# One sum and one reciprocal for a pair of heads, and a fixed place in the load queue for late weights and keys

## Chip, cores and metric

The kernel runs on one core of one Trainium2 chip. The metric is the device time of an execution in microseconds (us). The engines are PE (TensorE, matmuls), DVE (VectorE), ACT (ScalarE), POOL (GpSimd) and SP (SyncE, which here issues all loads and stores as one queue).

## The reference

Four batches with eight heads each: 512 local and 32 global queries and keys, head size 64. Local queries see the 32 global keys and the local keys within 32 positions; global queries see all keys. Then two MLPs over 2176 rows of 512.

```
s_g = scale * q_g @ k_all.T;   out_g = softmax(s_g) @ v_all
s_l = scale * [q_l @ k_g.T, where(|i - j| <= 32, q_l @ k_l.T, -1e9)]
out_l = softmax(s_l) @ [v_g, v_l]
x = rows of all heads side by side                    # 2176 x 512
h = maximum(x @ w_in, 0);      x2 = (h * h) @ w_out     # 512 -> 2048 -> 512
y = ((x2 @ w1) * (x2 @ w2)) @ w3 @ w_out2               # 512 -> 1024 -> 512
```

softmax here subtracts the row's maximum, takes exp, and divides by the sum plus 1e-9.

## The kernel before, in words

Heads go in 16 pairs j (heads 2j and 2j + 1); pairs 0 to 3 are batch 0, and so on. `emit_s(j, part)` makes the local scores of both heads of a pair for one half of the queries (part 0 or 1): for each head two tiles `sc`, 192 and 224 keys wide. `soft(i, part, sc)` (L235) turns one head's scores into probabilities `p`: for each tile DVE adds the mask, scales and takes the least (L245), and ACT takes the exponential and its row sum into `st` (L249). Then DVE adds each sum and the 1e-9 beside it (L253), takes the reciprocal (L254), and multiplies both tiles with it (L257). PE transposes `p` (`emit_t`, L332), ACT copies the result to `pt` (L334, L337), and PE multiplies it with v (`emit_pv`, tile `o`, L159); ACT copies `o` to `xb` (L363) and casts it to the high part `hl` (L584), DVE makes the low part (L154). The five `p` buffers and six `st` tiles are used in turn.

`emit_g(j)` does the 32 global queries of both heads at once: scores `sg` (L165), two maxima (L300), the larger of them (L303), its product with minus the scale (L304), exp on ACT (L306), sum, reciprocal and product (L309 to L311, tile `pg`), then transposes (`tg`, L319).

The MLP is in three products of high and low parts. First `h` (L165) from `hl` and the weights `u`, then `x` or `acc` (L165, L633). Later stages, with lines from L830 on, form both further products. Raw weights are 64-bit words, loaded by `load_w` (L447, `n` counts them) and converted in steps: two on ACT (L453, L456), two on DVE (L464, L469), an add on POOL (L536), a cast on ACT (L477) and a subtraction on DVE (L478). Attention of batch b + 1 runs beside the first MLP of batch b, and the conversions of units 0 to 15 beside both.

Keys and queries of pair j come by `load_kq` (L197): for pairs 4 to 7 straight into the tile that is used, for pairs 8 to 15 (j >= NATIVE) into `kqraw`, two buffers, which DVE splits into high and low parts (cast L228, subtraction L154, `kq_hl`).

What sets the order: the program is written as lists of steps that are merged, and a scheduler then orders the instructions of each engine by its own model of their times. An instruction under `tc.keep_in_program_order` keeps its place among those of its engine that are so marked. Each engine then runs its list strictly in order. All loads and stores are on one list too, that of SP; an issue waits until its tile is free or its data are there, and the issues behind it wait with it.

Of the kernel before, what the change touches and what calls it, by code (L numbers as in the profile page):

```python
# [9 lines left out]
F32 = mybir.dt.float32  # L10
F32R = mybir.dt.float32r
BF16 = mybir.dt.bfloat16
I32 = mybir.dt.int32
U32 = mybir.dt.uint32
AF = mybir.ActivationFunctionType
ALU = mybir.AluOpType
AX = mybir.AxisListType
# [4 lines left out]
S = SL + SG  # L22
# [3 lines left out]
SCALE = 0.125  # L26
# [13 lines left out]
NK = KPOS.size  # L40
KSTART = (0, 96, 256, 320)
# [3 lines left out]
REACH = ((0, 192), (96, 320), (256, 480), (384, 576))  # L45
SLOT = (0, 1, 1, 0)
WIDTH, AT, PW = (192, 224), (288, 0), 544
# [10 lines left out]
HALF = 256  # L58
# [12 lines left out]
RUNS = (0, 16, PAIRED + 16)  # L71
# [4 lines left out]
HEAD, FEW = 4, 2  # L76
# [31 lines left out]
NATIVE = 8  # L108
# [6 lines left out]
AT_BUFS, H_BUFS, X_BUFS, P_BUFS, KQ_BUFS, ST_BUFS, HL_BUFS = 4, 2, 2, 5, 4, 6, 14  # L115
# [3 lines left out]
def attention_mlp(ctx: ExitStack, tc: tile.TileContext, kq0, kq, vw, wts, mask, ident, out_d):  # L119
    nc = tc.nc  # L120
# [9 lines left out]
    cv, rot, at = cv_cm.__enter__(), rot_cm.__enter__(), at_cm.__enter__()  # L130
# [4 lines left out]
    mask_sb = rot.tile([128, 4, 256], BF16, name="mask_sb")  # L135
# [4 lines left out]


    p_all = [rot.tile([128, PW], F32, name=f"p{k}") for k in range(P_BUFS)]
    sts = [rot.tile([128, 10], F32, name=f"st{k}") for k in range(ST_BUFS)]
    stgs = [rot.tile([64, 8], F32, name=f"stg{k}") for k in range(2)]
    xs_d = dram.tile([128, 4, 2, NT], F32, name="xs_d")
    part_d = dram.tile([128, 4, NT], F32, name="part_d")
# [9 lines left out]
    def in_turn(products, whole):  # L156

        for k, (o, w, x, start, stop) in enumerate(products):
            m = mm(o, w, x, start=start, stop=stop)  # L159
            if k or whole:  # L160
                tc.keep_in_program_order(m)

    def chain(o, terms):
        for k, (w, x) in enumerate(terms):
            mm(o, w, x, start=(k == 0), stop=(k == len(terms) - 1))  # L165
# [16 lines left out]
    kq_raw, kq_t, v_t, p_t, pt_t = {}, {}, {}, {}, {}  # L182

    def kq_tile(name, dtype=F32):
        return rot.tile([128, S + NK], dtype, tag="kq", name=name, bufs=KQ_BUFS)
# [11 lines left out]
    def load_kq(j):  # L197

        if H <= 2 * j < B * H:
            if j < NATIVE:  # L200
                t = kq_tile("kq_f32")
            else:
                t = pools["cv"].tile([128, S + NK], F32, tag="kqraw", name="kqraw", bufs=2)
            kq_raw[j] = t
            for h, r in enumerate(ROWS):
                src = kq[2 * j + h - H, r]
                nc.sync.dma_start(out=t[r, :HALF], in_=src[:, :HALF])
                nc.sync.dma_start(out=t[r, HALF:S], in_=src[:, HALF + NK :])
                nc.sync.dma_start(out=t[r, S:], in_=src[:, HALF : HALF + NK])

    def load_v(i, part=None):

# [19 lines left out]
            kq_t[j, part] = [(both[a][0], both[e][1]) for a, e in PASSES]  # L232
        load_kq(j + 1)

    def soft(i, part, sc):  # L235

        p = p_all[0]
        p_all.append(p_all.pop(0))
        st = sts[(2 * i + part) % ST_BUFS]
        least, sums, over = st[:, 0:2], st[:, 2:6].rearrange("p (n k) -> p n k", k=2), st[:, 6:8]  # L240
        for t in range(2 * part, 2 * part + 2):
            n = SLOT[t]
            c, w = slice(AT[n], AT[n] + WIDTH[n]), slice(0, WIDTH[n])
            m = slice(REACH[t][0] - KSTART[t], REACH[t][1] - KSTART[t])
            nc.vector.tensor_tensor_reduce(  # L245
                out=p[:, c], in0=sc[:, n, w], in1=mask_sb[:, t, m], scale=-SCALE,
                scalar=3.0e38, op0=ALU.add, op1=ALU.min, accum_out=least[:, n : n + 1],
            )
            nc.scalar.activation(  # L249
                p[:, c], p[:, c], AF.Exp, bias=least[:, n : n + 1], scale=-1.0,  # L250
                accum_out=sums[:, n, 0:1],
            )
        nc.vector.tensor_reduce(out=over, in_=sums, axis=AX.X, op=ALU.add)  # L253
        nc.vector.reciprocal(over, over)  # L254
        for n in range(2):
            c = slice(AT[n], AT[n] + WIDTH[n])
            nc.vector.tensor_scalar_mul(p[:, c], p[:, c], over[:, n : n + 1])  # L257
        p_t[i, part] = p

    def emit_s(j, part):  # L260

        terms = kq_t[j, part]
        sc = [ps.tile([128, 2, 256], F32, tag="at", name="sc", bufs=AT_BUFS) for _ in ROWS]
        at_q, at_t = (128 * n + SG * part for n in range(2)), range(2 * part, 2 * part + 2)
        in_turn(
            (
                (o[:, n, : WIDTH[n]], x[r, c : c + 128], y[r, slice(*REACH[t])], k == 0, k == len(terms) - 1)
                for c, t, n in ((c, t, SLOT[t]) for c, t in zip(at_q, at_t))
                for k, (x, y) in enumerate(terms) for o, r in ((sc[h], ROWS[h]) for h in HEADS)
            ),  # L270
            j >= WHOLE,
        )
        for h, o in enumerate(sc):
            soft(2 * j + h, part, o)

    def emit_g(j):

        terms = kq_t[j, 1]
        qs = qgf if len(terms) == 1 else [qgp[:, 0], qgp[:, 0], qgp[:, 1]]
        for q, (x, _) in list(zip(qs, terms))[:: 2]:  # L280
            for h, r in enumerate(ROWS):
                nc.gpsimd.tensor_copy(q[r, SG * h : SG * (h + 1)], x[r, :SG])
        bank = dict(tag="x", bufs=X_BUFS) if j < APART else dict(tag="at", bufs=AT_BUFS)
        sg = [ps.tile([128, 512], F32, name="sg", **bank) for _ in range(2)]

        pf = pg.rearrange("p c k -> p (c k)")
        tail = pf[:, 288:736].rearrange("p (a c) -> p a c", a=2)[:, :, :128]
        pieces = (
            (sg[0][:, :288], lambda x: x[:, :288], pf[:, :288]),
            (  # L290
                sg[1][:, :256].rearrange("p (a c) -> p a c", a=2),
                lambda x: x[:, 256:576].rearrange("p (a c) -> p a c", a=2)[:, :, 32:160],
                tail,
            ),
        )
        for k, (s, of_keys, _) in enumerate(pieces):
            chain(s, [(q, of_keys(y)) for q, (_, y) in zip(qs, terms)])
        st = stgs[j % 2]
        for k in range(2):
            nc.vector.tensor_reduce(  # L300
                out=st[:, k : k + 1], in_=sg[k][:64, : 256 + 32 * (1 - k)], axis=AX.X, op=ALU.max
            )
        nc.vector.tensor_reduce(out=st[:, 2:3], in_=st[:, 0:2], axis=AX.X, op=ALU.max)  # L303
        nc.vector.tensor_scalar_mul(st[:, 2:3], st[:, 2:3], -SCALE)  # L304
        for k, (s, _, p) in enumerate(pieces):
            nc.scalar.activation(  # L306
                p[:64], s[:64], AF.Exp, bias=st[:, 2:3], scale=SCALE, accum_out=st[:, 3 + k : 4 + k]
            )
        nc.vector.tensor_reduce(out=st[:, 6:7], in_=st[:, 3:6], axis=AX.X, op=ALU.add)  # L309
        nc.vector.reciprocal(st[:, 6:7], st[:, 6:7])  # L310
        nc.vector.tensor_scalar_mul(pf[:64, :640], pf[:64, :640], st[:, 6:7])  # L311
# [77 lines left out]
    def cycle(j, ahead=True, behind=True):  # L389
# [3 lines left out]
        if ahead:  # L393
            s.append(lambda: (emit_k(n) if n == H // 2 else None, emit_g(n)))
            s += [lambda part=part: emit_s(n, part) for part in ((1,) if native else (0, 1))]
# [39 lines left out]
    def load_w(n):  # L435
        if n < RUNS[1]:
            t = unit("u1", I32).rearrange("p a c -> p (a c)").rearrange("p (c w) -> p c w", w=2)
        elif n % 3 == 2:
            t = extra["w"][:, :1024].bitcast(I32).rearrange("p (c w) -> p c w", w=2)
        else:  # L440
            t = pools["cv"].tile([128, 512, 2], I32, tag="wraw", name="wraw", bufs=2)
        if n >= PAIRED:
            k, u = divmod(n - PAIRED, 2)
            at = PAIRED + 2 * (LATE + FIRST)[k] + u
        else:
            at = ORDERED[n] if n < RUNS[1] else n
        nc.sync.dma_start(out=t, in_=wts[at].bitcast(I32).rearrange("p (c w) -> p c w", w=2))  # L447
        raw_t[n] = t

    def conv_a(n):  # L450
# [22 lines left out]
    def unit(tag, dtype=F32R):  # L473
        return pools[tag].tile([128, 2, 512], dtype, tag=tag, name=tag, bufs=16)
# [239 lines left out]
    def end_a(i, d, o):  # L714
        (nc.scalar.copy if d < 2 or i < SHARED else nc.vector.tensor_copy)(staged(i, d), o)
        if d == 3:
            nc.sync.dma_start(out=of(part_d, i), in_=st_t[0])

    def split_a(i, d):
        if i < NBLK:  # L720
            split_x(i, d, xcols(i)[:, d])
        else:
            load_split(0, d, 2)
# [20 lines left out]
    for i in range(0, NBLK, 2):  # L744
        main = []
        for j in (i, i + 1):
            if j >= SHARED:
                if j == SHARED:
# [3 lines left out]
                    lambda d, j=j: split_a(j + 1, d), lambda d, j=j: end_a(j, d, acc[d]),  # L752
# [15 lines left out]
        else:  # L768
# [9 lines left out]
            for j in range(FEW):  # L778
# [3 lines left out]
                    lambda d, j=j: end_few(j, d),  # L782
# [190 lines left out]
    for i in range(NBLK):  # L973
# [3 lines left out]
            lambda d, i=i: end_b(i, d), 0 if i < NBLK - 1 else 4,  # L977
# [243 lines left out]
```

## Time and profile before

| | |
|---|---|
| median of 3 runs | 853.44 us (851.83 to 854.47) |
| profiled execution, device time | 852.59 us |
| its span, first to last instruction | 850.8 us |
| mean granted clock of PE | 0.994 of 2.4 GHz |
| busy: PE, DVE, ACT, POOL | 826.6, 587.9, 491.1, 216.5 us |
| loads and stores | 151.96 MB, 54.0% of the 16 DMA engines' time in the main queue |

A row of the page gives an engine's busy time and the number of its instructions. A timeline gives each instruction's start and length; instructions of one kind in a row are merged to one line with their number. In square brackets stands how long the engine was idle before, and what ended that. The chain of work that ended last is, for its last 86 us, PE alone.

### The profile page before, as it was taken

Reading aid. Unit: us, or ns where it says so; the run is one execution under the profiler, and the core shown is the slowest. Engines: PE = TensorE matmul, PEld = TensorE weight load, DVE = VectorE, ACT = ScalarE, POOL = GpSimd, SP = SyncE. Lnnn points to the kernel's source line nnn. Section 1 sums busy time; section 2 is a strip of 40 time slices with the busy share of each in tenths; the row PEclk is TensorE's granted clock in tenths of the full one; section 3 lists DMA queues with packets and bytes.
Section 4 is the critical chain, followed back from the end, with each engine's and each line's share of the span. In section 5 each row is a group of like instructions: output and inputs, shape, how many; then the busy total and the mean of one; then the engine's idle time right before and its main releaser. Section 6 shows DMA issues by size and latency. Waiting matters only on the chain. (4 is left out here: it accounts for less than half of the span.)

```text
span 850.8 us, 17854 instructions
## 1 busy us (share of the span) xinstructions
PE 826.6 (97%) x6624; PEld 787.8 (93%) x6624; DVE 587.9 (69%) x1611; ACT 491.1 (58%) x1323; POOL 216.5 (25%) x256
## 2 busy tenths in 40 slices
PE   6789799999999999999999999999999999999998
PEld 4578689999999999999999999999999999999998
DVE  7878986773866576877662027796896757789862
ACT  7778876664766787777664246776411212255650
POOL 3401222000200233333331003330277454442000
PEclk9999999999999999999999999999999999999999
DMA  9964313424051685875854239745347543939931
GB/s 335 262 197 144 114 54 118 133 78 127 29 174 33 228 279 180 284 253 182 252 153 157 69 120 330 248 167 174 128 140 242 195 145 111 333 114 331 336 142 54
DMA packets 89879, 151.96 MB, mean 179 GB/s; under 512 B 6336, under 2 KB 63296, under 8 KB 89792
## 3 DMA queue, kind: packets, MB, share of 16 engines
q1 hardware_dynamic: 89792, 150.82, 54.0%
q8 instruction: 52, 0.85, 0.4%
q14 instruction: 35, 0.29, 0.1%
HBM read 103.42 MB, written 47.38 MB: 177 GB/s over the span
## 5 line engine op out<-in xcount | busy, mean ns | idle before, releaser
L165 PE MATMUL h<-hl,u 128*128 128x288 f32 (+1 forms) x1536 | 229.3, 292 | 2.6 <-ACT hl L584 1.1
L165 PEld LDWEIGHTS h<-hl,u 128*128 128x128 f32 x1536 | 205.6, 190 | 8.6 <-ACT hl L584 1.3
L830 PE MATMUL m<-hl,u 128*128 128x272 f32 x1296 | 170.9, 288 | 0.9 <-DVE r L852 0.9
L830 PEld LDWEIGHTS m<-hl,u 128*128 128x128 f32 x1296 | 165.3, 188 | 1.4 <-ACT hl L866 1.1
L633 PE MATMUL acc<-hl,u 128*128 128x256 f32 (+1 forms) x1032 | 149.0, 288 | 0.2 <-DVE hl L154 0.2
L633 PEld LDWEIGHTS acc<-hl,u 128*128 128x128 f32 x1032 | 137.6, 188 | 1.2 <-DVE hl L154 0.4
L154 DVE TENSOR_TENSOR hl<-r,hl 128x288 fp32r<-128x288 f32 (+1 forms) x128 | 80.1, 630 | 73.8 <-ACT r L604 72.6
L536 POOL TENSOR_TENSOR wt<-wt 128x512 int32<-128x512 int32 x56 | 74.0, 1322 | 213.6 <-DVE wt L469 72.6
L599 ACT ACTIVATE r<-h 128x288 f32<-128x288 f32 (+1 forms) x128 | 49.9, 393 | 75.4 <-PE h L165 74.2
L165 PE MATMUL x<-hl,u 128*128 128x288 f32 (+1 forms) x504 | 74.0, 294 | 0.0
L847 ACT COPY r<-m 128x272 f32<-128x272 f32 x40 | 15.4, 385 | 101.0 <-PE m L830 96.1
L249 ACT ACTIVATE p<-p,st 128x192 f32<-128x192 f32 (+1 forms) x128 | 59.0, 464 | 19.5 <-DVE st L245 19.3
L830 PE MATMUL m<-u,u 128*128 128x272 f32 x528 | 70.0, 287 | 0.0
L165 PEld LDWEIGHTS x<-hl,u 128*128 128x128 f32 x504 | 66.6, 189 | 2.5 <-issue 1.3
L830 PEld LDWEIGHTS m<-u,u 128*128 128x128 f32 x528 | 67.2, 188 | 0.3 <-DVE rs L854 0.2
L478 DVE TENSOR_TENSOR u<-wt,u 128x512 fp32r<-128x512 f32 x56 | 40.3, 719 | 29.6 <-ACT u L477 29.0
L600 ACT ACTIVATE hl<-r 128x288 fp32r<-128x288 f32 (+1 forms) x128 | 54.8, 432 | 4.2 <-PE acc L633 1.5
L1023 POOL TENSOR_TENSOR rs<-rs 128x272 f32<-128x272 f32 x64 | 55.7, 881 | 3.2
L1022 POOL TENSOR_TENSOR rs<-rs 128x272 f32<-128x272 f32 x32 | 28.7, 898 | 98.9 <-DVE rs L860 98.9
L245 DVE CUSTOM_DVE_ANT_0 p<-sc,mask_sb 128x192 f32<-128x192 f32 (+1 forms) x128 | 40.8, 368 | 14.6 <-PE sc L159 14.5
L469 DVE SCALAR_TENSOR_TENSOR wt<-wt 128x512 int32<-128x512 int32 x72 | 49.6, 689 | 1.7
L526 POOL TENSOR_TENSOR u<-wt 128x512 int32<-128x512 int32 x16 | 22.5, 1410 | 99.0 <-DVE wt L469 81.9
(113 smaller groups left out, 1271.0 us busy)
## 6 DMA issues: line engine op xcount, KB each, us to landing
wraw<-in_wts SPq DMA_DIRECT2D x37, 512.0 KB, 4.3
q_d<-rs SPq DMA_DIRECT2D x16, 952.0 KB, 4.6
rl<-q_d SPq DMA_DIRECT2D x12, 1088.0 KB, 7.4
wx<-in_wts SPq DMA_DIRECT2D x19, 512.0 KB, 5.1
u<-in_wts SPq DMA_DIRECT2D x16, 512.0 KB, 6.3
v_f<-in_vw SPq DMA_DIRECT2D x24, 256.0 KB, 3.0
hl<-xs_d SPq DMA_DIRECT2D x20, 288.0 KB, 4.4
hl<-xs_d SPq DMA_DIRECT2D x20, 256.0 KB, 4.3
```

Source lines behind the costliest of these rows:

```text
L154: eng.tensor_tensor(out=lo, in0=raw, in1=hi.bitcast(F32), op=ALU.subtract)
L165: mm(o, w, x, start=(k == 0), stop=(k == len(terms) - 1))
L245: nc.vector.tensor_tensor_reduce(out=p[:, c], in0=sc[:, n, w], in1=mask_sb[:, t, m], scale=-SCALE, scalar=3.0e38, op0=ALU.add, op1=ALU.min ...
L249: nc.scalar.activation(p[:, c], p[:, c], AF.Exp, bias=least[:, n : n + 1], scale=-1.0, accum_out=sums[:, n, 0:1],)
L469: nc.vector.scalar_tensor_tensor(out=b, in0=a, scalar=-(1 << 31), in1=b, op0=ALU.bitwise_and, op1=ALU.bitwise_or)
L478: s = nc.vector.tensor_tensor(out=t[:, 1, cols], in0=raw, in1=t[:, 0, cols].bitcast(F32), op=ALU.subtract)
L536: nc.gpsimd.tensor_tensor(out=b, in0=b, in1=m, op=ALU.add)
L599: nc.scalar.activation(r, h, AF.Relu)
L600: nc.scalar.activation(g[:, 0], r, AF.Square)
L633: mm(acc[d], w[:, a, 128 * d : 128 * (d + 1)], g_t[f][:, b], start=(f + k == 0), stop=(last and k == 2),)
L830: mm(o, w, x, start=(i in (1, 6, 5, 4) and k == 0), stop=(k == len(terms) - 1), skip_group_check=(i in (2, 7, 3)),)
L1023: sub = lambda o, a, c: nc.gpsimd.tensor_tensor(out=o, in0=a, in1=c, op=ALU.subtract)
```

## The change

`soft` now takes a pair, not a head. The four tiles of the two heads have their four row sums in one `st` tile, sixteen columns wide instead of ten; one sum over all four and one reciprocal follow, then the four multiplications. In `emit_g`, the larger of two maxima and its product with minus the scale become one instruction. Loads of raw weights 8 to 15 and of the keys of pairs 8 to 15 are marked to keep the program's order. The diff, without lines that only carry a new argument:

```diff
-    sts = [rot.tile([128, 10], F32, name=f"st{k}") for k in range(ST_BUFS)]
+    sts = [rot.tile([128, 16], F32, name=f"st{k}") for k in range(ST_BUFS)]
...
-                nc.sync.dma_start(out=t[r, :HALF], in_=src[:, :HALF])
-                nc.sync.dma_start(out=t[r, HALF:S], in_=src[:, HALF + NK :])
-                nc.sync.dma_start(out=t[r, S:], in_=src[:, HALF : HALF + NK])
+                q, k = slice(0, HALF), slice(HALF, HALF + NK)
+                for to, c in ((q, q), (slice(HALF, S), slice(HALF + NK, None)), (slice(S, None), k)):
+                    d = nc.sync.dma_start(out=t[r, to], in_=src[:, c])
+                    if j >= NATIVE:
+                        tc.keep_in_program_order(d)
...
-    def soft(i, part, sc):
-
-        p = p_all[0]
-        p_all.append(p_all.pop(0))
-        st = sts[(2 * i + part) % ST_BUFS]
-        least, sums, over = st[:, 0:2], st[:, 2:6].rearrange("p (n k) -> p n k", k=2), st[:, 6:8]
-        for t in range(2 * part, 2 * part + 2):
...
+    def soft(j, part, scs):
+
+        st = sts[(2 * j + part) % ST_BUFS]
+        least, sums = st[:, 0:4], st[:, 4:12].rearrange("p (n k) -> p n k", k=2)
+        over, cols = st[:, 12:16], [slice(AT[n], AT[n] + WIDTH[n]) for n in range(2)]
+        for h, sc in enumerate(scs):
+            p = p_t[2 * j + h, part] = p_all[0]
+            p_all.append(p_all.pop(0))
+            for t in range(2 * part, 2 * part + 2):
+                n = SLOT[t]
+                k, c, w = 2 * h + n, cols[n], slice(0, WIDTH[n])
...
         nc.vector.tensor_reduce(out=over, in_=sums, axis=AX.X, op=ALU.add)
         nc.vector.reciprocal(over, over)
-        for n in range(2):
-            c = slice(AT[n], AT[n] + WIDTH[n])
-            nc.vector.tensor_scalar_mul(p[:, c], p[:, c], over[:, n : n + 1])
-        p_t[i, part] = p
+        for h in range(2):
+            for n, c in enumerate(cols):
+                p, k = p_t[2 * j + h, part], 2 * h + n
+                nc.vector.tensor_scalar_mul(p[:, c], p[:, c], over[:, k : k + 1])
...
-        for h, o in enumerate(sc):
-            soft(2 * j + h, part, o)
+        soft(j, part, sc)
...
-        nc.vector.tensor_reduce(out=st[:, 2:3], in_=st[:, 0:2], axis=AX.X, op=ALU.max)
-        nc.vector.tensor_scalar_mul(st[:, 2:3], st[:, 2:3], -SCALE)
+        nc.vector.tensor_scalar(
+            out=st[:, 2:3], in0=st[:, 0:1], scalar1=st[:, 1:2], scalar2=-SCALE, op0=ALU.max, op1=ALU.mult
+        )
...
-        nc.sync.dma_start(out=t, in_=wts[at].bitcast(I32).rearrange("p (c w) -> p c w", w=2))
+        d = nc.sync.dma_start(out=t, in_=wts[at].bitcast(I32).rearrange("p (c w) -> p c w", w=2))
+        if 2 * HEAD <= n < RUNS[1]:
+            tc.keep_in_program_order(d)
```

The scheduler orders all engines anew. Three places of its lists follow, each as it stood and as it stands.

DVE, the softmax of the third pair of batch 0 (part 0), whose probabilities are `p_84` and `p_80`; `u` and `wt` are weights in conversion. Before, line numbers of the kernel before:

```order
L245 ISA p_81,st_85<-sc,mask_sb 128x192
L245 ISA st_85 128x1
L245 ISA p_81,st_85<-sc,mask_sb 128x224
L245 ISA st_85 128x1
L469 SCALAR_TENSOR_TENSOR wt<-wt 128x512
L253 TENSOR_REDUCE st_87<-st_87 128x2
L245 ISA p_82,st_87<-sc,mask_sb 128x224
L245 ISA st_87 128x1
L254 RECIPROCAL st_87<-st_87 128x2
L478 TENSOR_TENSOR u_486<-wt,u_486 128x512
L257 TENSOR_SCALAR p_84<-p_84,st_87 128x192
L257 TENSOR_SCALAR p_84<-p_84,st_87 128x224
```

Now, with the changed kernel's line numbers (L257 is the sum, L258 the reciprocal, L262 the multiplication, L303 the maximum over global scores):

```order
L249 ISA p_81,st_85<-sc,mask_sb 128x192
L249 ISA st_85 128x1
L249 ISA p_81,st_85<-sc,mask_sb 128x224
L249 ISA st_85 128x1
L257 TENSOR_REDUCE st_89<-st_89 128x4
L258 RECIPROCAL st_89<-st_89 128x4
L303 TENSOR_REDUCE stg_91<-sg 64x1
L262 TENSOR_SCALAR p_84<-p_84,st_89 128x192
L262 TENSOR_SCALAR p_84<-p_84,st_89 128x224
L262 TENSOR_SCALAR p_80<-p_80,st_89 128x192
L262 TENSOR_SCALAR p_80<-p_80,st_89 128x224
```

Two steps of weight conversion stood between the fourth pair's scores and the multiplication of `p_84`; now none does, and one pass over the global scores does. The multiplication of `p_80` stood earlier, and now follows.

SP, the load queue after the second halves of batch 0's keys (`kq_f`). Before:

```order
L193 DMA kq_f_118<-in_kq 128x512
L207 DMA kqraw<-in_kq 64x256
L208 DMA kqraw<-in_kq 64x288
L209 DMA kqraw<-in_kq 64x576
L207 DMA kqraw<-in_kq 64x256
L447 DMA u_303<-in_wts 128x1024
L208 DMA kqraw<-in_kq 64x288
L209 DMA kqraw<-in_kq 64x576
L207 DMA kqraw<-in_kq 64x256
L447 DMA u_345<-in_wts 128x1024
```

Now:

```order
L193 DMA kq_f_118<-in_kq 128x512
L451 DMA u_295<-in_wts 128x1024
L219 DMA v_f_308<-in_vw 128x256
L219 DMA v_f_310<-in_vw 128x256
L451 DMA u_337<-in_wts 128x1024
L219 DMA v_f_349<-in_vw 128x256
L219 DMA v_f_351<-in_vw 128x256
L592 DMA xs_d<-hl 128x2x256
```

Twelve loads of the keys of pairs 8 and 9 stood among those of raw weights 7 to 9; now they stand some sixty places further down, the six of pair 8 behind the store of the first block's partial sums (`part_d`), two loads of v and the load of raw weight 15, the six of pair 9 behind those and two more loads of v.

DVE, at the global softmax of pair 6 (`pg`, the seventh). Before:

```order
L154 TENSOR_TENSOR hl<-r,hl 128x288
L309 TENSOR_REDUCE stg_91<-stg_91 64x1
L478 TENSOR_TENSOR u_1391<-wt,u_1391 128x512
L464 TENSOR_SCALAR wt<-wt 128x512
L300 TENSOR_REDUCE stg_92<-sg 64x1
L310 RECIPROCAL stg_91<-stg_91 64x1
L300 TENSOR_REDUCE stg_92<-sg 64x1
L469 SCALAR_TENSOR_TENSOR wt<-wt 128x512
L311 TENSOR_SCALAR pg<-pg,stg_91 64x640
```

Now (L313 to L315 are the sum, reciprocal and product of the global softmax, L230 the keys' cast, L484 and L470 steps of weight conversion):

```order
L154 TENSOR_TENSOR hl<-r,hl 128x288
L313 TENSOR_REDUCE stg_91<-stg_91 64x1
L314 RECIPROCAL stg_91<-stg_91 64x1
L315 TENSOR_SCALAR pg<-pg,stg_91 64x640
L230 CAST kq_hl<-kqraw 128x1120
L484 TENSOR_TENSOR u_1355<-wt,u_1355 128x512
L303 TENSOR_REDUCE stg_92<-sg 64x1
L470 TENSOR_SCALAR wt<-wt 128x512
L303 TENSOR_REDUCE stg_92<-sg 64x1
L154 TENSOR_TENSOR kq_hl<-kqraw,kq_hl 128x1120
```

Three steps of weight conversion and two maxima stood between the sum and the product; now nothing does. The cast of pair 8's keys, which stood far ahead, now stands right behind it.

## Rows read from the trace of the kernel before

**Rows 1.** The page, first part: span, then busy time of PE and DVE.

```profile
span 850.8 us, 17854 instructions
...
PE 826.6 (97%) x6624; PEld 787.8 (93%) x6624; DVE 587.9 (69%) x1611; ACT 491.1 (58%) x1323; POOL 216.5 (25%) x256
```

**Rows 2.** Busy time (instructions) of each engine in two stretches, granted clock, DMA.

```profile
core 0: us, PE busy (x) PEld busy (x) DVE busy (x) ACT busy (x) POOL busy (x), PEclk, DMA share, GB/s
80.00:110.00 30.00, 25.72 (x222) 22.43 (x221) 29.96 (x112) 26.93 (x85) 6.96 (x9) 0.94 0.26 82
170.00:255.00 85.00, 85.00 (x799) 79.79 (x797) 55.97 (x231) 53.21 (x176) 7.99 (x16) 1.00 0.32 101
```

**Rows 3.** PE's timeline: start, length, instructions, idle time before and what ended it.

```profile
26.58 1.51 PE L332 MATMUL tp<-ident_sb,p 128*128 128x128 f32 x6 [2.85 <-DVE p L257]
...
34.20 1.09 PE L159 MATMUL o<-pt_f,v_f 128*64 128x128 f32 x16 [0.78 <-DMA v_f<-in_vw]
...
40.73 0.50 PE L165 MATMUL h<-hl,u 128*128 128x256 f32 x2 [1.10 <-ACT hl L584]
...
55.02 1.09 PE L332 MATMUL tp<-ident_sb,p 128*128 128x128 f32 x8 [2.00 <-DVE p L257]
...
103.43 0.33 PE L319 MATMUL tg<-ident_sb,pg 64*128 64x64 f32 x2 [2.39 <-DVE st L253]
```

**Rows 4.** Stretches as in rows 2, behind three groups of gaps.

```profile
26.00:30.00 4.00, 3.42 (x24) 2.93 (x25) 4.00 (x16) 2.25 (x6) 1.74 (x3) 0.57 1.03 277
42.00:48.00 6.00, 5.80 (x31) 4.84 (x31) 4.50 (x20) 3.75 (x15) 0.41 (x2) 0.72 0.97 334
104.00:108.00 4.00, 4.00 (x28) 3.06 (x28) 3.96 (x18) 4.00 (x14) 0.50 (x1) 0.59 0.00 0
```

**Rows 5.** Instructions by line and form: count, busy us, mean ns, idle before.

```profile
L469 DVE SCALAR_TENSOR_TENSOR wt<-wt 128x512 int32<-128x512 int32 x72 | 49.6, 689 | 1.7
...
L478 DVE TENSOR_TENSOR u<-wt,u 128x512 fp32r<-128x512 f32 x56 | 40.3, 719 | 29.6 <-ACT u L477 29.0
...
L254 DVE RECIPROCAL st<-st 128x2 f32<-128x2 f32 x64 | 10.0, 158 | 0.9
...
L253 DVE TENSOR_REDUCE st<-st 128x2 f32<-128x4 f32 x64 | 9.3, 148 | 10.1 <-ACT p L249 10.0
...
L300 DVE TENSOR_REDUCE stg<-sg 64x1 f32<-64x288 f32 x16 | 7.1, 445 | 6.8 <-PE sg L165 6.7
...
L303 DVE TENSOR_REDUCE stg<-stg 64x1 f32<-64x2 f32 x16 | 2.2, 139 | 0.2
...
L536 POOL TENSOR_TENSOR wt<-wt 128x512 int32<-128x512 int32 x56 | 74.0, 1322 | 213.6 <-DVE wt L469 72.6 <-issue 44.6 <-ACT hl L600 33.0
```

**Rows 6.** DVE's timeline at the third pair's softmax and at the seventh global one.

```profile
24.58 1.62 DVE L478 TENSOR_TENSOR u<-wt,u 128x512 fp32r<-128x512 f32 x1
...
26.12 0.55 DVE L257 TENSOR_SCALAR p<-p,st 128x192 f32<-128x192 f32 x2
...
28.48 1.36 DVE L257 TENSOR_SCALAR p<-p,st 128x192 f32<-128x192 f32 x2
...
102.84 0.54 DVE L311 TENSOR_SCALAR pg<-pg,stg 64x640 f32<-64x640 f32 x1
```

**Rows 7.** The load queue (SPq): start, length and number of issues.

```profile
14.47 0.59 SPq L207 DMA_DIRECT2D kqraw<-in_kq  x1
...
27.23 0.47 SPq L209 DMA_DIRECT2D kqraw<-in_kq  x1
...
87.83 0.60 SPq L717 DMA_DIRECT2D part_d<-st  x1
...
95.06 1.00 SPq L217 DMA_DIRECT2D v_f<-in_vw  x2
```

**Rows 8.** ACT's timeline, a weight cast that waits for POOL.

```profile
38.79 0.62 ACT L477 CAST u<-wt 128x512 fp32r<-128x512 f32 x1 [2.40 <-POOL wt L536]
```

**Rows 9.** All kqraw loads: time from issue to landing.

```profile
DMA to landing us min/median/max: 2.1/3.0/8.1
```

More of the change, by code (lines that the diff above doesn't have):

```diff
@@ L233, in emit_k @@
         load_kq(j + 1)
-    def soft(i, part, sc):
-        p = p_all[0]
-        p_all.append(p_all.pop(0))
-        st = sts[(2 * i + part) % ST_BUFS]
-        least, sums, over = st[:, 0:2], st[:, 2:6].rearrange("p (n k) -> p n k", k=2), st[:, 6:8]
-        for t in range(2 * part, 2 * part + 2):
[L242 to L252, printed above, removed]
+    def soft(j, part, scs):
[8 more added lines that the diff above has]
+                k, c, w = 2 * h + n, cols[n], slice(0, WIDTH[n])
+                m = slice(REACH[t][0] - KSTART[t], REACH[t][1] - KSTART[t])
+                nc.vector.tensor_tensor_reduce(
+                    out=p[:, c], in0=sc[:, n, w], in1=mask_sb[:, t, m], scale=-SCALE,
+                    scalar=3.0e38, op0=ALU.add, op1=ALU.min, accum_out=least[:, k : k + 1],
+                )
+                nc.scalar.activation(
+                    p[:, c], p[:, c], AF.Exp, bias=least[:, k : k + 1], scale=-1.0,
+                    accum_out=sums[:, k, 0:1],
+                )
@@ L302, in emit_g @@
             )
-        nc.vector.tensor_reduce(out=st[:, 2:3], in_=st[:, 0:2], axis=AX.X, op=ALU.max)
-        nc.vector.tensor_scalar_mul(st[:, 2:3], st[:, 2:3], -SCALE)
+        nc.vector.tensor_scalar(
+            out=st[:, 2:3], in0=st[:, 0:1], scalar1=st[:, 1:2], scalar2=-SCALE, op0=ALU.max, op1=ALU.mult
+        )
         for k, (s, _, p) in enumerate(pieces):
```

## The prediction

> **What bounds the kernel now.** I read the page's first part, then busy time by stretches, then PE's timeline with the idle time before each instruction. PE is busy for 826.6 of 850.8 us [rows 1], and between 170 and 255 us for 85.00 of 85.00 at the full clock [rows 2]; the stretches after it read alike. So a gain has to come out of the 24.2 us in which PE is idle, or out of stretches at the low clock, and both lie early, where softmax runs. In PE's timeline the gaps stand in brackets [rows 3]: 2.85 us before the transposes at 26.58, 0.78 and 1.10 at 34 and 41, 2.00 at 55, and 2.39 before 103.43; from 80 to 110 us PE is idle for 30.00 - 25.72 = 4.28 us in all, while VectorE (DVE) is busy for 29.96 [rows 2]. All the gaps named but the 0.78 (a load of v) end with DVE or ScalarE (ACT). Behind three groups of gaps the granted clock falls from 2.4 towards 1.2 GHz: it averages 0.57 over 26 to 30 us, 0.72 over 42 to 48, and 0.59 over 104 to 108 [rows 4]. At full clock the same work would take 4 x 0.43 = 1.72, 6 x 0.28 = 1.68 and 4 x 0.41 = 1.64 us less. In two of these three stretches DVE is busy all the time.
>
> The sum below is made against the profiled execution, 852.59 us; the median of the runs, 853.44, is 0.85 above it.
>
> **What is removed.** 32 of 64 sums (148 ns each) and 32 of 64 reciprocals (158 ns) go, and 16 of 32 small steps of the global softmax (139 ns) [rows 5]: 9.8 + 2.2 = 12.0 us of DVE. The sum and the reciprocal that stay are four columns wide instead of two. No row has that shape; between "no longer" and "twice as long" (32 x 306 ns = 9.8 us, which would give it all back) I take the first, because the sum of two columns into one on 64 rows costs 139 ns and that of four into two on 128 rows 148. Of the 12.0 us only what stands ahead of something PE waits for counts; after 170 us it is hidden under PE and I cost it at nothing. If that cover went, it could only gain.
>
> **What is moved.** This is worth more than what is removed, and the order listing shows it.
>
> *a. The third pair's transposes (the gap of 2.85).* Before, a weight split that starts at 24.58 and lasts 1.62 us goes ahead of the multiplication at 26.12, for which PE waits [rows 6]. Now that split stands behind the multiplications. Ahead of them there are also three sums and three reciprocals fewer (3 x 0.31 = 0.9 us) and one pass over global scores more (445 ns; both by [rows 5]). So the multiplication comes 1.62 + 0.9 - 0.4 = 2.1 us earlier, and the second head's multiplication, some 0.5 us, moves behind as well: 2.6 at most. I take -2.4; the ends are -2.85 (all of the gap) and 0.
>
> *b. Gaps of 0.78 and 1.10.* The v load that PE waits for at 34 us stands behind twelve loads of keys for pairs 8 and 9, issued from 14.47 to 27.23 us [rows 7]; these now go behind all of the early weights. The 1.10 ends with ACT's copy, which was behind a weight cast that waited 2.40 us for POOL [rows 8]; the listing has that unit's conversion later on both engines. Ends 0 and -1.88, taken -1.3.
>
> *c. The clock.* The low stretches at 26 and 104 us each follow a gap that a or e closes: -1.72 - 1.64 = -3.4. The one at 42 I leave. Ends 0 and -5.0.
>
> *d. A new wait, at the second pair.* The pair's sum now needs all four exponentials, and on ACT the last two stand behind a copy (before: ahead of it), while DVE has the third pair's scores between sum and reciprocal. PE's transposes of pair 2 then wait for what they did not wait for before. Not in the trace; the nearest row is the wait of 2.00 at 55 us, for a chain of the same make [rows 3], and here only the last two exponentials are new: between 0 and 2.0 I take +0.7. For the first pair both heads' sums end within the time that the first transposes wait anyway: nothing. At 55 us the chain is scores, four exponentials, sum, multiplication; one sum fewer against a pair's wait: 0, ends -1.0 and +1.0.
>
> *e. The gaps of 4.28 from 80 to 110 us.* DVE is saturated there [rows 2]. The 2.39 among them ends with the global probabilities' multiplication at 102.84 [rows 6], and now a weight conversion (its two longer steps 689 + 719 ns [rows 5]), one step of a key split and several sums no longer stand ahead of it. By counting the rows of the listing with their mean durations, it now comes over 6 us of DVE's work sooner behind pair 10's scores, and so do the multiplications of pair 12. I take -3.3; ends 0 and -4.28.
>
> *f. Keys of pair 8, late.* Their loads are now issued behind the store of the first block, two loads of v and the last raw weight; before, that store left at 87.83 and those v at 95.06 [rows 7], with the keys long there. Six issues at 0.47 to 0.59 us and a landing of 3.0 us (median; largest 8.1) [rows 7, 9] follow. DVE's cast stands in order behind the seventh global multiplication, and behind the cast are pair 13's sum and pair 14's scores. I cannot tell from the trace which comes first; ends 0 and 8.1 - 3.0 = +5.1. I take +1.0, nearest to the wait of 2.00 at 55 us, which is of the same make, halved because DVE runs late there. The other key loads keep two buffers and over ten microseconds.
>
> Sum: -2.4 - 1.3 - 3.4 + 0.7 - 3.3 + 1.0 = -8.7. 852.59 - 8.7 = 843.9 for a profiled execution, **844.7 us** for the median.
>
> **The rivals.**
>
> *1. The conversions that were put off hold up softmax.* Three of them (units 6 to 8 in order of conversion) now lie between some 48 and 65 us. Each has an add on POOL, 1322 ns [rows 5]. When that add runs beside a DVE instruction, rows differ: 1.62 us for a split whose mean is 719 ns, and 1.36 us for a multiplication of two pieces that takes 0.55 at 26.12 [rows 5, 6]. Three adds of up to 1.32 us in front of multiplications make up to +4.0: 848.7 us. For it: PE waits there already (2.00 at 55). Against: DVE has the slack. The Trainium skill (SBUF — State Buffer, section "SBUF: two separate sides") says that GpSimd and DVE share one pair of ports under an exclusive lock, whoever starts first keeping it for the whole instruction; by that rule a block costs up to a whole add and the sum would be the 848.7 above, where the forecast has 0 for it; the two rows that ran 0.8 to 0.9 us over agree with it.
>
> *2. Same within the measurement.* ACT is nearly as full as DVE from 80 to 110 us, 26.93 of 30 [rows 2], and loses no work by the change. If ACT takes the place of DVE in every wait, the gaps stay: 853.4. Against: only one gap of those listed has ACT at its end.
>
> *3. Slower.* The same late conversions, but standing ahead of the sums of pairs 6, 7 and 8: per pair 1.41 us for a unit's two longer steps [rows 5] and 0.9 of contention, 2.3 us; three times 6.9, and the clock falls behind each as it did three times before, 1.72 + 1.68 + 1.64 = 5.0 [rows 4]: 11.9 - 8.7 = +3.2 on the median, **856.6 us**. It decides once these waits and the low clock behind them come to more than 8.7 us, some 2.9 for each pair. Against: the listing has them behind the multiplications of pairs 6 and 7.
>
> *4. The pinned loads do nothing.* Only 0.78 us of PE's gaps end with a load after the start, so pinning by itself is worth that at most; then b shrinks and the forecast stays within a microsecond.
>
> **How the numbers follow.** Forecast (839.4 to 848): 0.60. Rival 1 (848 to 850.9): 0.19. Better than 839.4, which needs every end at once (-2.85 - 1.88 - 5.0 - 4.28 = -14.0): 0.03. Same, rival 2: 0.10; 0.3% is 2.6 us, about what a measurement of this kernel can tell from no change. Slower, rival 3 or a worse f: 0.08. Faster is 0.60 + 0.19 + 0.03 = 0.82. The range runs from 839.0 to 851.5; it leaves out some 0.03 below and 0.16 above. Rival 4 shares the forecast's time and has no chance of its own.
>
> **What would show it.** In the changed profile: the wait before the third pair's transposes under 1 us; no granted clock under 0.9 around 28 and 105; the wait of the global transposes near 103 gone; DVE busy 575 to 577 us instead of 587.9 [rows 1] if the wide sum costs no more. It is wrong if DVE's cast of pair 8 waits for its keys by over 3 us with PE idle behind it, or if new waits on p of over 2 us stand between 48 and 70 us.

## The result, and the profile after

The changed kernel takes 845.73 us (median of 4 runs, 844.68 to 846.67); the kernel before, beside it, 852.63 us (851.28 to 854.47). The ratio is 0.9912, with a 95% interval of 0.9898 to 0.9926: faster by 0.9% (by the two medians 6.9 us, 0.8%). The profiled execution, of 846.67 us, is the slowest of the four.

The first lines of its page answer to [rows 1]:

```profile
span 844.9 us, 17768 instructions
...
PE 822.7 (97%) x6624; PEld 785.2 (93%) x6624; DVE 580.0 (69%) x1531; ACT 491.1 (58%) x1323; POOL 210.8 (25%) x256
```

The span is 5.9 us shorter. PE does the same 6624 matmuls in 3.9 us less, so most of the gain is clock. Busy time by stretches shows where, beside [rows 2, 4] (after the stretch and its length: PE, PEld, DVE, ACT, POOL, granted clock, DMA share, GB/s):

```profile
26.00:30.00 4.00, 4.00 (x40) 3.54 (x39) 3.90 (x15) 4.00 (x12) 0.30 (x2) 1.00 0.55 185
42.00:48.00 6.00, 4.39 (x51) 3.62 (x50) 5.66 (x25) 5.21 (x21) 0.41 (x2) 1.00 0.52 148
104.00:108.00 4.00, 4.00 (x30) 3.61 (x30) 3.51 (x8) 2.21 (x5) 1.47 (x1) 1.00 0.26 88
100.00:110.00 10.00, 9.73 (x60) 8.89 (x61) 8.85 (x30) 6.93 (x21) 1.56 (x1) 0.84 0.36 108
80.00:110.00 30.00, 25.00 (x212) 21.84 (x211) 27.37 (x91) 23.74 (x73) 8.13 (x10) 0.94 0.45 127
10.00:110.00 100.00, 89.19 (x737) 74.27 (x738) 87.41 (x316) 84.78 (x266) 23.32 (x32) 0.98 0.64 198
```

The low clock at 26 and 42 us is gone. The third fall is not; it has moved to an earlier time: 104 to 108 us are at full clock now, but 100 to 110 us still at 0.84. The same row of the kernel before for the first hundred microseconds:

```profile
10.00:110.00 100.00, 86.89 (x692) 71.35 (x692) 86.50 (x335) 81.73 (x256) 23.33 (x32) 0.95 0.64 195
```

From these rows comes a small ledger for 10 to 110 us. PE idle: 13.11 us before, 10.81 now, -2.3. Clock: 1.72 + 1.68 + 1.64 = 5.0 us lost before [rows 4], 10 x 0.16 = 1.6 now, -3.4 (an estimate: the length of a stretch times what its clock lacks). Together -5.7, near the -5.9 of the span.

PE's timeline, the gaps that answer to [rows 3]:

```profile
16.95 1.51 PE L336 MATMUL tp<-ident_sb,p 128*128 128x128 f32 x6 [1.82 <-ACT wt L462]
25.69 0.85 PE L336 MATMUL tp<-ident_sb,p 128*128 128x128 f32 x6 [0.43 <-DVE p L262]
47.27 0.65 PE L336 MATMUL tp<-ident_sb,p 128*128 128x128 f32 x4 [1.60 <-DVE p L262]
54.56 0.66 PE L336 MATMUL tp<-ident_sb,p 128*128 128x128 f32 x4 [1.12 <-DVE p L262]
92.36 0.33 PE L323 MATMUL tg<-ident_sb,pg 64*128 64x64 f32 x2 [1.10 <-DVE pg L315]
94.69 2.30 PE L159 MATMUL o<-pt_f,v_f 128*64 128x160 f32 x36 [1.05 <-ACT pt_f L338]
100.27 1.65 PE L165 MATMUL h<-hl,u 128*128 128x256 f32 x6 [2.86 <-DVE hl L154]
```

The wait before the third pair's transposes fell from 2.85 to 0.43 us, and those of 0.78 and 1.10 are gone. A new one of 1.82 stands before the second pair's. Between 80 and 110 us PE is idle for 5.00 us, not 4.28, and the longest gap, 2.86, ends with DVE. What DVE did ahead of it:

```profile
91.76 0.55 DVE L315 TENSOR_SCALAR pg<-pg,stg 64x640 f32<-64x640 f32 x1
93.68 0.74 DVE L230 CAST kq_hl<-kqraw 128x1120 fp32r<-128x1120 f32 x1 [1.38 <-DMA kqraw<-in_kq]
...
95.98 1.30 DVE L154 TENSOR_TENSOR kq_hl<-kqraw,kq_hl 128x1120 fp32r<-128x1120 f32 x1
...
99.81 0.41 DVE L154 TENSOR_TENSOR hl<-xb,hl 128x256 fp32r<-128x256 f32 x1
```

and the load queue, which answers to [rows 7]:

```profile
83.19 0.60 SPq L723 DMA_DIRECT2D part_d<-st  x1
84.04 1.27 SPq L219 DMA_DIRECT2D v_f<-in_vw  x2
85.36 0.50 SPq L451 DMA_DIRECT2D u<-in_wts  x1
85.91 3.70 SPq L209 DMA_DIRECT2D kqraw<-in_kq  x6
```

Pair 8's keys are issued behind the block's store, two v and a weight. The chain of work that ended last runs through them, up to the split:

```profile
89.01 4.45 DMA kqraw<-in_kq
...
93.68 0.06 DVE kq_hl L230
```

DVE waits 1.38 us for them, and then the split of these keys stands ahead of what PE needs. In the kernel before, its cast came long before this stretch, and its subtraction in it:

```profile
76.98 0.74 DVE L228 CAST kq_hl<-kqraw 128x1120 fp32r<-128x1120 f32 x1
...
90.53 1.32 DVE L154 TENSOR_TENSOR kq_hl<-kqraw,kq_hl 128x1120 fp32r<-128x1120 f32 x1
```

Last, the small steps, in DVE's groups by form, beside [rows 5]:

```profile
L258 DVE RECIPROCAL st<-st 128x4 f32<-128x4 f32 x32 | 5.5, 173 | 0.7
L257 DVE TENSOR_REDUCE st<-st 128x4 f32<-128x8 f32 x32 | 4.9, 154 | 20.9 <-ACT p L253 20.6
...
L306 DVE TENSOR_SCALAR stg<-stg 64x1 f32<-64x1 f32 x16 | 3.2, 200 | 0.2
```

Four columns cost 6 and 15 ns more than two: the wide form is all but free.

### The profile page after: what moved, and what is told of

It reads as the page before. It is cut to its first block, busy times and chain, and to the rows that moved or that the text cites. A ratio compares the mean times of both kernels' runs of the same rounds, so it can differ in the third digit from the quotient of the medians.

```text
span 844.9 us, 17768 instructions
## 1 busy us (share of the span) xinstructions
PE 822.7 (97%) x6624; PEld 785.2 (93%) x6624; DVE 580.0 (69%) x1531; ACT 491.1 (58%) x1323; POOL 210.8 (25%) x256
## 4 chain that ended last, share of the span: by engine, by line
PE 89%; ACT 3%; DVE 3%; DMA 2%; issue 1%; SPq 1%; POOL 1%; DVEq 0%; POOLq 0%; ACTq 0%
PE m L836 30%; PE h L165 21%; PE acc L639 14%; PE x L165 8%; PE wacc L804 5%; PE o L159 4%; PE sc L159 3%; PE tp L336 3%; PE sg L165 1%; DMA x2l<-x_d 1%; ACT u L483 1%; PE tg L323 1%; DMA kqraw<-in_kq 1%; ACT hl L872 1%; ACT p L253 1%
## 5 line engine op out<-in xcount | busy, mean ns | idle before, releaser
L253 ACT ACTIVATE p<-p,st 128x224 f32<-128x224 f32 (+1 forms) x128 | 59.1, 466 | 21.2 <-DVE st L249 21.2
L484 DVE TENSOR_TENSOR u<-wt,u 128x512 fp32r<-128x512 f32 x56 | 38.5, 689 | 27.7 <-ACT u L483 27.1
L475 DVE SCALAR_TENSOR_TENSOR wt<-wt 128x512 int32<-128x512 int32 x72 | 51.5, 716 | 1.8
L249 DVE CUSTOM_DVE_ANT_0 p<-sc,mask_sb 128x224 f32<-128x224 f32 (+1 forms) x128 | 40.7, 368 | 15.9 <-PE sc L159 15.8
L804 PE MATMUL wacc<-u,u 128*128 128x512 f32 x192 | 47.3, 392 | 0.0
```

The costliest lines, as they stand in the source:

```text
L253: nc.scalar.activation(p[:, c], p[:, c], AF.Exp, bias=least[:, k : k + 1], scale=-1.0, accum_out=sums[:, k, 0:1],)
L475: nc.vector.scalar_tensor_tensor(out=b, in0=a, scalar=-(1 << 31), in1=b, op0=ALU.bitwise_and, op1=ALU.bitwise_or)
L804: mm(o, w3[:, a, 128 * q : 128 * (q + 1)], w_t[32 + 4 * half + q][:, b], start=(half + q + k == 0), stop=(half + q + k == 6),)
```

## The experiments

All ratios are against runs of the kernel before on the same chip, with medians from 853.05 to 853.25 us. Kernels 1 to 4, 5 to 8, 9 to 11 and 12 ran on four different chips, so a difference between two of these groups also goes across chips. Kernels named by a change to "the changed kernel" have everything else as it has.

**1 to 4: each half alone, and pair 8's keys early.** The first kernel has no marks (two edits, this and the same for the weights), the second has only the marks:

```diff
-                    if j >= NATIVE:
-                        tc.keep_in_program_order(d)
```

> The changed kernel with the marks on the loads taken away: keys of pairs 8 and 9 load early again, softmax by pairs and the merged step of the global softmax stay. If the merged softmax and the DVE order that it brings are the cause of the gain (theory): 846 us, within 2 of the changed kernel, with the wait before the third pair's transposes (2.85 us before, 0.43 in the changed kernel) under 1 us; and if the late keys of pair 8 are what keeps the waits between 80 and 104 us, some 843 to 845. If the marks are the cause (rival): 851 to 853, with gaps of 2 us or more back before 45 us.

> The kernel before with only the marks on the loads of late weights and keys: softmax head by head as before. If the merged softmax is the cause (theory): 851 to 854 us, with the gap of about 2.9 us near 26 us still there and DVE busy for 587 to 589 us. If taking twelve loads of keys out of the early queue is the cause (rival): 846 to 848, the gaps of 0.78 and 1.10 us near 34 and 41 us gone.

Measured: merged softmax alone 849.71 us, ratio 0.9955 (0.9942 to 0.9967); marks alone 850.31, 0.9964 (0.9952 to 0.9977). Neither expectation held for either kernel: each half carries about half of the gain. The merged softmax alone has no gap at the third pair, but one at the next, behind a weight conversion, and a late v. PE's timeline of that kernel:

```profile
30.94 0.41 PE L334 MATMUL tp<-ident_sb,p 128*128 128x128 f32 x2 [2.08 <-DVE p L260]
38.30 1.09 PE L159 MATMUL o<-pt_f,v_f 128*64 128x128 f32 x16 [1.38 <-DMA v_f<-in_vw]
```

From 80 to 110 us, though, this kernel leaves PE idle for 1.69 us only, at full clock, with the split of pair 8's keys about where it stood before (cast at 75.64, subtraction at 89.87 us):

```profile
80.00:110.00 30.00, 28.31 (x241) 24.30 (x240) 29.70 (x106) 27.33 (x85) 8.78 (x8) 1.00 0.43 121
```

Marks alone keep the gap near 26 us (2.12 us) with a clock of 0.57 behind it, and lose the gaps at 34 and 41.

The third kernel leaves pair 8's keys free; the fourth marks them two pairs earlier:

```diff
-                    if j >= NATIVE:
+                    if j > NATIVE:
```

```diff
+        if j == 6:
+            load_kq(NATIVE)
-        if H <= 2 * j < B * H:
+        if H <= 2 * j < B * H and j not in kq_raw:
```

> The changed kernel with the marks on the keys of pairs 9 to 15 only; those of pair 8 load early again, before 30 us. If the late keys of pair 8 hold up DVE near 94 us and through it PE near 100 us (theory): DVE's wait of 1.38 us for kqraw is gone, the gap of 2.86 us before the products h at 100 us falls under 1, and so does the fall of the clock behind it: 845.7 - 2 - 1.6 = 842 us, within 1.5. If DVE's own load keeps those gaps (rival): 845 to 847, with a gap of 2 us or more still between 98 and 105 us. Early loads may also cost up to 0.8 us near 34 us, in either case.

> The changed kernel with the six loads of pair 8's keys marked two pairs earlier in the program, so that they stand in the load queue ahead of the store of the first block and not behind it. Theory: as with the free loads of pair 8, but nothing added near 34 us: 841 to 843 us, DVE's wait for kqraw gone, the gap near 100 us under 1 us. Rival, DVE's own load: 845 to 847 with the gap still there.

Measured: 842.48 us, 0.9875 (0.9862 to 0.9889), and 842.21 us, 0.9867 (0.9852 to 0.9882). The intervals lie below that of the changed kernel, and the theory holds. The fourth kernel's DVE timeline has the cast where DVE has time to spare (16.36 of 20 us busy from 60 to 80) and the subtraction at the end of that stretch, both without a wait:

```profile
70.69 0.74 DVE L232 CAST kq_hl<-kqraw 128x1120 fp32r<-128x1120 f32 x1
...
79.85 1.31 DVE L154 TENSOR_TENSOR kq_hl<-kqraw,kq_hl 128x1120 fp32r<-128x1120 f32 x1
```

Its PE timeline has no gap over 1.2 us between 80 and 135 us, and its stretches no low clock:

```profile
92.69 0.33 PE L325 MATMUL tg<-ident_sb,pg 64*128 64x64 f32 x2 [1.18 <-DVE pg L317]
94.81 2.30 PE L159 MATMUL o<-pt_f,v_f 128*64 128x160 f32 x36 [0.83 <-ACT pt_f L340]
```

```profile
80.00:110.00 30.00, 27.94 (x246) 24.10 (x245) 29.04 (x98) 27.47 (x85) 8.70 (x9) 1.00 0.35 108
10.00:110.00 100.00, 92.16 (x770) 76.49 (x771) 89.74 (x329) 88.53 (x279) 24.79 (x33) 1.00 0.63 198
```

Idle 7.84 instead of 10.81 us and no clock lost: -3.0 - 1.6 = -4.6 against the changed kernel's profile, where the span differs by 4.0.

**5: which marks gain.** The kernel before, with the marks on raw weights 8 to 15 only:

```diff
+        if 2 * HEAD <= n < RUNS[1]:
+            tc.keep_in_program_order(d)
```

> The kernel before with the marks on the loads of raw weights 8 to 15 only; the keys are free and load early as before. If the marks gain because weights that load later put off the conversions on ACT, DVE and POOL (theory): 850 to 851 us, like the marks on both, with the gap of 1.10 us near 41 us gone. If they gain because twelve loads of keys leave the early queue (rival): 852.5 to 854, the gaps near 34 and 41 us still there.

Measured: 850.40 us, 0.997 (0.996 to 0.9979), the same as with both marks. The theory's time held, and the gap of 1.10 is gone, though one of 0.91 for ACT's r stands near it. So the marks on the weights give the whole gain of kernel 2, and those on the keys add nothing to it that can be measured. Two things make up the gain. The clock from 42 to 48 us is back, 6 x 0.28 = 1.7 us, and PE is idle for 12.27 us between 10 and 110 us instead of 13.11. From 30 to 36 us DVE, ACT and POOL all have less to do. The first row is of the kernel before, the others are of kernel 5:

```profile
30.00:36.00 6.00, 4.99 (x40) 3.72 (x39) 5.57 (x16) 5.97 (x16) 3.49 (x3) 1.00 1.00 284
30.00:36.00 6.00, 6.00 (x60) 5.04 (x60) 2.96 (x9) 4.53 (x11) 1.69 (x3) 1.00 0.55 181
42.00:48.00 6.00, 5.89 (x66) 5.23 (x65) 5.79 (x24) 4.99 (x16) 0.45 (x1) 1.00 0.61 173
```

The load of v that PE waited for comes sooner too, though the keys still stand ahead of it, with two weight loads gone from the queue before it; the wait of 0.78 us for it is gone. The load queue, before and then in kernel 5:

```profile
28.08 1.93 SPq L217 DMA_DIRECT2D v_f<-in_vw  x2
```

```profile
26.58 1.13 SPq L217 DMA_DIRECT2D v_f<-in_vw  x2
```

No run tells apart what the earlier v and what the later conversions give. POOL's timeline shows the conversions' additions of these weights; first before, then with the marks:

```profile
28.21 1.27 POOL L536 TENSOR_TENSOR wt<-wt 128x512 int32<-128x512 int32 x1 [1.68 <-DVE wt L469]
32.45 1.27 POOL L536 TENSOR_TENSOR wt<-wt 128x512 int32<-128x512 int32 x1 [2.97 <-DVE stg L309]
...
37.49 1.26 POOL L536 TENSOR_TENSOR wt<-wt 128x512 int32<-128x512 int32 x1
```

```profile
30.70 1.28 POOL L538 TENSOR_TENSOR wt<-wt 128x512 int32<-128x512 int32 x1 [4.51 <-DVE stg L310]
...
40.80 1.65 POOL L538 TENSOR_TENSOR wt<-wt 128x512 int32<-128x512 int32 x1
```

Three conversions between 28 and 39 us became one by then: a mark on a load puts off the work that needs it, on three engines.

**6: the new wait at the second pair.** The fourth kernel, with sum and reciprocal by heads for that pair alone (`two` is one head's two columns):

```diff
+            if (j, part) == (1, 0):
+                two = slice(2 * h, 2 * h + 2)
+                nc.vector.tensor_reduce(out=over[:, two], in_=sums[:, two], axis=AX.X, op=ALU.add)
+                nc.vector.reciprocal(over[:, two], over[:, two])
```

> The kernel with pair 8's keys marked two pairs earlier (842.21 us), with sum and reciprocal head by head again for the second pair of batch 0 alone. If the new wait of 1.8 us before the second pair's transposes is lost time (theory, term d): 840 to 841.3 us, that wait under 0.7 us and PE's next ones no longer by as much. If PE only waits later for the third pair instead, whose steps on DVE come behind (rival): 841.8 to 843.

Measured: 844.84 us, 0.9904 (0.9891 to 0.9917). Both were wrong: slower by 2.6 us, and the wait grew. PE's timeline:

```profile
19.01 1.51 PE L343 MATMUL tp<-ident_sb,p 128*128 128x128 f32 x6 [3.96 <-DVE p L269]
```

The new order put the first head's sum and reciprocal early and the second head's multiplication behind more scores and a conversion. The scheduler ordered everything anew, so one pair could not be edited alone; the kernel says nothing on the price of that wait.

**7, 8, 10 and 11: the two merged steps, one at a time.** Two sums for a pair (the lines of kernel 6 for all pairs, in 7 and 11), and the global softmax's two small steps apart again (8 and 10), each from the changed kernel and from the fourth:

```diff
-        nc.vector.tensor_scalar(
-            out=st[:, 2:3], in0=st[:, 0:1], scalar1=st[:, 1:2], scalar2=-SCALE, op0=ALU.max, op1=ALU.mult
-        )
+        nc.vector.tensor_reduce(out=st[:, 2:3], in_=st[:, 0:2], axis=AX.X, op=ALU.max)
+        nc.vector.tensor_scalar_mul(st[:, 2:3], st[:, 2:3], -SCALE)
```

> The changed kernel with two sums and two reciprocals, one for each head, in the softmax of a pair (128x2 as before); the marks and the merged step of the global softmax stay. If one sum for a pair is what brings the merged part's gain, by its fewer steps and the order of DVE that follows (theory): 849.5 to 851 us, like the marks alone (850.31). If it is the merged step of the global softmax (rival): 845 to 847. DVE busy 584 to 587 us either way.

> The changed kernel with the two small steps of the global softmax apart again, as before the change; one sum and reciprocal for a pair and the marks stay. If one sum for a pair carries the merged part's gain (theory): 845 to 847 us, within 1 of the changed kernel. If the merged step of the global softmax carries it (rival): 849 to 851. DVE busy 581 to 583 us either way.

> The kernel with pair 8's keys two pairs earlier (842.21 us), with the two small steps of the global softmax apart again. If the 2.4 us that this cost in the changed kernel were the late keys of pair 8 (DVE waited 3.14 us for them there, ahead of the global multiplication) and not the step (theory): 842 to 843 us and no gap of over 1.5 us between 90 and 100 us. If the merged step itself saves time (rival): 844 to 845.

> The kernel with pair 8's keys two pairs earlier (842.21 us), with two sums and two reciprocals, one for each head. If one sum for a pair gains in the first 60 us and the late keys of pair 8 hid a part of that gain in the changed kernel (theory): 845.5 to 848 us, with PE clocked down between 24 and 30 us. If its gain was only that it moved what waits for pair 8's keys (rival): 842 to 844.

Measured: two sums 847.89 us, 0.994 (0.9927 to 0.9953), and with pair 8's keys early 845.26, 0.9906 (0.9893 to 0.992). Global steps apart 848.14, 0.9935 (0.992 to 0.995), and with the keys early 843.14, 0.9883 (0.9869 to 0.9896). From the changed kernel the two cost about the same, 2.2 and 2.4 us, and no theory had that; the interval of kernel 8 still touches that of the changed kernel. From the fourth kernel it is 3.0 and 0.9 us, just outside both theories' ranges; the 3.0 is clear, but the intervals of kernel 10 and the fourth kernel overlap, so the 0.9 is not told apart from nothing. So one sum for a pair is the larger part, and most of the 2.4 was probably not the small step. DVE's timeline of that kernel (8) shows what was:

```profile
95.07 0.74 DVE L230 CAST kq_hl<-kqraw 128x1120 fp32r<-128x1120 f32 x1 [3.14 <-DMA kqraw<-in_kq]
95.73 0.54 DVE L314 TENSOR_SCALAR pg<-pg,stg 64x640 f32<-64x640 f32 x1
```

The cast, which waits 3.14 us there, had come to stand ahead of the global multiplication, and PE waited 4.26 us for that one. In kernel 11 the clock was expected down between 24 and 30 us; it was 1.00 there, and 0.86 from 48 to 60. DVE was busy for 582.0 us in kernel 7 and 575.1 in kernel 8, under the expected bounds.

**9: marks on the weights only,** with the merged steps: the changed kernel with the edit of kernel 1 for the keys alone.

> The changed kernel with the marks on raw weights 8 to 15 only; all keys are free. If the marks on the weights give all that marks give, and those on the keys only cost (theory): 842 to 843.2 us, like the kernels with pair 8's keys early (842.48 and 842.21), no wait for kqraw on DVE before 100 us. If the keys of pair 9 have to be out of the early queue as well (rival): 844 to 846, with a gap of some 0.8 to 1.4 us for a load of v between 30 and 40 us.

Measured: 843.21 us (841.64 to 844.65), 0.9882 (0.9866 to 0.9898): by its time the theory, though not told apart from a microsecond more. Its profiled execution, the slowest, has a gap of 1.39 us for v at 35.69 as the rival had it, but there the first loads came 1.7 us late too. Whether early keys of pair 9 hold up v stays open. What is clear: without the marks on keys nothing is lost; it is 2.5 us faster than the changed kernel.

**12: POOL beside DVE.** The fourth kernel with two of POOL's additions cut short:

```diff
-        nc.gpsimd.tensor_tensor(out=b, in0=b, in1=m, op=ALU.add)
+        w = slice(0, 4 if n in (1, 2) else 512)
+        nc.gpsimd.tensor_tensor(out=b[:, w], in0=b[:, w], in1=m[:, w], op=ALU.add)
```

> The kernel with pair 8's keys two pairs earlier (842.21 us), with POOL's additions for the second and third raw weight done on 4 of 512 columns only; the rest of these two additions is left out, so that these weights come out wrong, and the order on DVE and ACT is the same until the second pair's transposes are past. If the new wait of 1.81 us before the second pair's transposes is as long as it is because POOL's additions stretch DVE's instructions beside them (theory): the conversion step that took 1.64 us in front of the second pair's sum takes 0.7, its four multiplications 1.0 instead of 1.64, the wait falls under 0.8 us, and the time to 840.8 to 841.7. If it is the late exponentials on ACT alone (rival): the wait stays over 1.4 us and the time within 0.5 of 842.2.

DVE's timeline around the second pair's softmax, first in the fourth kernel, then here:

```profile
13.75 1.64 DVE L477 SCALAR_TENSOR_TENSOR wt<-wt 128x512 int32<-128x512 int32 x1
...
16.03 1.64 DVE L264 TENSOR_SCALAR p<-p,st 128x192 f32<-128x192 f32 x4
```

```profile
13.39 0.69 DVE L477 SCALAR_TENSOR_TENSOR wt<-wt 128x512 int32<-128x512 int32 x1
...
14.99 1.04 DVE L264 TENSOR_SCALAR p<-p,st 128x192 f32<-128x192 f32 x4
```

The addition beside the first of these steps starts at 13.45 us in the fourth kernel and lasts 1.39 us, and starts at 13.09 and lasts 0.32 here. PE's timeline here:

```profile
15.46 1.51 PE L338 MATMUL tp<-ident_sb,p 128*128 128x128 f32 x6 [0.52 <-ACT u L485]
27.42 0.41 PE L338 MATMUL tp<-ident_sb,p 128*128 128x128 f32 x2 [1.40 <-DVE p L264]
```

At the place itself everything came as the theory had it: 1.64 to 0.69, 1.64 to 1.04, and the wait from 1.81 to 0.52 us. The time did not. Expected at 840.8 to 841.7, it was 843.98 us, 0.9892 (0.9876 to 0.9909), 1.8 more than the fourth kernel. The order behind that place is another one; a wait of 1.40 stands at 27 us, and the clock averages 0.91 from 80 to 100 us (20 x 0.09 = 1.8 us).

## Why the prediction was right, and where not

The forecast, 844.7 us, was 1.0 us under the measured 845.73, and its sum of -8.7 us was too large by some 3 us against the profiled execution (-5.9) and by 1.8 against the two medians (-6.9). That the time came so near is partly luck: the kernel before took 0.8 us less beside the changed one than in the runs that the forecast started from, and c's figure is right although two of its three places came out otherwise. Term by term:

- **a** (-2.4) held: 2.85 to 0.43 us.
- **b** (-1.3): both gaps went, -1.9. But rival 4's sentence that "pinning by itself is worth that at most", 0.78 us, was wrong. The marks alone gave 2.9 us. Rival 4 counted only the wait for v, and not the other gap and the low clock behind it, which went as well once weight loads and their conversions came later (experiment 5).
- **c** (-3.4) came to -3.4, with two places wrong that cancel: the fall at 42 us, which I left, went (-1.68), and the one at 104, which I took away, stayed in another form (1.64 before, 1.6 now).
- **d** (+0.7) was too small: 1.82 us, where before PE waited 0.46 us near there, for scores: +1.4. The pair's last exponential stands behind a copy and two weight steps, as read in the order; what I had not priced is that two of POOL's additions lie just there. Experiment 12 shows that they stretch DVE's steps, and that most of the wait is theirs: with them cut short 0.52 us is left, near the 0.46 of before. So little remains for what d was to price, the sum that waits for four exponentials. This is rival 1's mechanism, at a place that I had not considered.
- At 55 us: 1.60 + 1.12 for 2.00, +0.7, within its ends.
- **e and f are the step that failed.** "I take -3.3" for the gaps of 80 to 110 us and "I take +1.0" for the late keys, -2.3 together, became +0.7: idle 5.00 for 4.28. With the keys early the idle time there is 30.00 - 27.94 = 2.06 us (kernel 4), and it is 1.69 in kernel 1, whose split stands about where it stood before. So e by itself is worth 2.2 to 2.6 of the 3.3, and the clock comes back as well. The late keys cost 845.73 - 842.21 = 3.5 us, not 1.0. I had priced only the wait for the landing, between 0 and 5.1, and the wait was 1.38. What I left out is the work behind it: the cast (0.74 us) and the subtraction (1.30), which came at 76.98 and 90.53 us before, now both stand between the landing and the step that PE waits for at 100.27. On PE the late keys show as 5.00 - 2.06 = 2.9 us of idle time and 1.6 of clock, together 4.5 where the spans differ by 4.0. The lengths 1.38 + 0.74 + 1.30 = 3.4 come near, but they are not measured shares: kernel 9's subtraction runs at 83.42 us, in the same full stretch, and PE is idle for 2.06 us there all the same.
- DVE's total, 575 to 577 us forecast, is 580.0. The wide sum and reciprocal cost 0.7 us more (32 x 21 ns), and the merged step takes 200 ns where the multiplication that was to stay took 136 (1.0 us). The other 2.4 us are not shown; how often DVE runs beside POOL may be the reason, as kernel 8, with sixteen more instructions, has 575.1.

Of the rivals, the times of 1 (848.7), 2 and 3 did not come; ACT took DVE's place only at one gap of about a microsecond. Rival 1 put three of POOL's additions between 48 and 65 us; the profile has one there, at 49.89, and the next at 76.40. The waits on p are 1.60 us at 47.27 and 1.12 at 54.56, under the 2 that would have shown the forecast wrong. Nor did the wait for the late keys exceed 3 us. Of the signs that were to show it right, the third pair's wait and the clock around 28 us came; the clock around 105 us (100 to 110 us average 0.84) and DVE's busy time did not, and of the global transposes' wait 1.10 us are left.

The Trainium skill's page SBUF — State Buffer, section "SBUF: two separate sides", on which rival 1 rested, says that DVE and GpSimd hold a shared pair of ports in turn, each for a whole instruction, where DVE's instruction has two inputs in SBUF or runs in a mode with two ports. Experiment 12 agrees with it in the lengths: with POOL's additions cut to 0.2 to 0.3 us, DVE's step beside them took 0.69 instead of 1.64 us. That the ports are the reason, no trace here shows.

The kernel with the lowest median here is the fourth, 842.21 us: the change with pair 8's keys marked two pairs earlier, 1.3% under the kernel before. The third, 842.48, is not told apart from it.

## What to carry to other kernels

When a load is put off, move the whole of what it feeds in your sum, not only its landing: here the late keys cost 3.5 us, of which DVE's wait for them was 1.4; the steps that split them then stood in a stretch where DVE was short. The same effect can gain where the work leaves a full stretch: marks on weight loads were worth 2.8 us, of which the wait for v, gone with them, was only 0.78. And count the clock beside the gaps: of 5.9 us, 3.4 were stretches at the lower level behind gaps of one to three microseconds.

## What was not expected of the hardware

Sum and reciprocal of four columns cost 154 and 173 ns, of two 148 and 158. An addition of 128x512 on POOL (1.3 to 1.4 us) made a DVE step of 0.69 take 1.64 us (experiment 12); the changed kernel has that length twice in its first 22 us, at 13.60 and 20.82. And two parts of a change that gain 3.5 us (merged softmax) and 2.8 us (marks on weights) alone give 9.8 together when the keys stay free (843.21 us): each alone keeps a gap of over 2 us before transposes in the first 31 us (2.08 in kernel 1, 2.20 in kernel 5), and together they have none over 1.9. Behind these gaps the clock falls (0.72 over 30 to 36 us in kernel 1, 0.57 over 26 to 30 in kernel 5), and in kernel 9 it stays at 1.00 from 10 to 110 us. That this is why the two gain more together was not tested.
